# Two heads' float32 attention products side by side in the first two batches of a sink-attention and mixer kernel

## The chip, the core and the metric

One Trainium2 chip, one core of it. The metric is the device time of one execution in microseconds. Five engines matter here: TensorE (PE, with its weight loads shown apart as PEld), VectorE (DVE), ScalarE (ACT), GpSimd (POOL), and SyncE (SP), which issues nearly all transfers.

## What is computed

Attention with 4 sink keys and a window of 128 keys, for 4 batches, 8 heads, 768 positions and a head size of 64; its output goes through a mixer: a rank-32 mix along the sequence and a feed-forward layer of 2048.

```python
def _attn_ref(q, k, v, n_sink, window):          # q, k, v: (4, 8, 768, 64)
    scores = scale * np.matmul(q, k.transpose(0, 1, 3, 2))
    keep = is_sink | in_window                   # 4 sinks, 128 keys back
    scores = np.where(keep, scores, -1000000000.0)
    a = np.exp(scores - max); a = a / (sum(a) + 1e-09)
    return np.matmul(a, v)
def _moe_ref(x, U, V, w_ch1, w_ch2):             # x: (4, 768, 512)
    u = x + (xt @ U @ V).transpose(0, 2, 1)
    return u + np.maximum(u @ w_ch1, 0.0) @ w_ch2
```

The weights come as 64-bit floats and are turned into pairs of reduced float32 tiles (fp32r, a high and a low part) on the chip, in seven steps each (`narrow_steps`, L83).

## The kernel before

The order of the work is written out by a planner. Each piece is a step with an engine (or a choice of engines), an assumed duration, a priority and the tiles that it reads and writes (`Plan.any`, L246). A list scheduler runs forward and backward over all steps, picks an engine where there is a choice, and the steps are then issued in the order of their planned starts (`order`, L271). Its durations are the code's own entries, not measurements.

Batch 0's attention runs first, by halves of the sequence (`attention_halves`, L788): 2 halves of 384 positions, 8 heads each. Then batch 0's feed-forward runs (`spread`, L1021, and `ffn`, L950), during which the weights are narrowed for the first time and batch 1's attention is done beside it (`attention`, L773). Batch 2's attention lies beside batch 1's feed-forward, and so on. A gate lets head h of batch 1 start only when the feed-forward has reached its mark int(6 + 2.5 h) (`BESIDE`, L64, and L779).

One head and half (`attend`, L766) takes: three score products, one for each block of 128 queries, over 260 columns of keys (132 for the first block of the sequence); for each a masked minimum on DVE (L643) and an exponential on ACT (L648); the normalising (L663 to L693); three transposes (L702); two triangular maskings of the transposed tile (DVE L711, POOL L727); and the product with the values (L752), whose result is copied from a PSUM bank into the activations xT (line L462 on ACT, L463 on DVE, both in the helper `copy`).

`WHOLE` (L61) says which products are plain float32: all of batches 0 and 1. There the scores use one float32 matmul over 128 rows, of which 64 are the head and 64 are zeros that the host put there (L637). The values' matmul takes 128 columns of stationary operand, of which 64 are the head and the other 64 the next block, not used (L751); the copy takes the first 64 rows of the result (L759). Batches 2 and 3 use fp32r pairs instead (L640, L641) and are not touched.

Loads for the plain products are one q, one k and one v transfer per head (`load_qk`, L611, `prep_v`, L571); heads take the tiles kh, qs, vhl or kl, qkraw, opl by turns. The first two heads' q and k are loaded ahead of the plan (L1283 to L1289), with zeros set by DVE on the other 64 rows.

Of the kernel before, what the change touches and what calls it, by code (L numbers as in the profile page):

```python
# [21 lines left out]
P = 128  # L22
# [8 lines left out]
NS = 4  # L31
# [25 lines left out]
NP = 3  # L57
NXT = NPAIR + 1
PERIOD = 4.32
ACC = (0xFFFF, 0xFFFF, 0xFFFF, 0xFFFF)  # L60
WHOLE = {0: (0xFFFF, 0xFFFF), 1: (0xFF, 0xFF)}  # L61
# [13 lines left out]
def f32(ap):  # L75
    return ap.bitcast(F32)

# [341 lines left out]
def dve(n):  # L419
    return 0.069 + n * 1.042e-3  # L420
# [14 lines left out]
class Fast:  # L435
# [135 lines left out]
    def prep_v(self, b, h, blocks, t0, whole=False):  # L571
# [5 lines left out]
        if whole:  # L577
            t = self.opl() if h % 2 else self.vhl()
            flat = lambda: f32(t().rearrange("p n s d -> p (n s d)")[:, :(n + 1) * D])
            self.put(t, lambda: (flat().rearrange("p (n d) -> p n d", n=n + 1), self.v[b, h][:, k0:k1 + 1, :]), (n + 1) * 32768, t0 - 8)  # L580
            return t, flat, k0
# [5 lines left out]
        return t, None, k0  # L587
# [23 lines left out]
    def load_qk(self, b, h, halves, t0):  # L611

        if b == 0 and halves == (0, 0) and h < len(self.first):
            qr, kr = self.first[h]
            return qr, kr, None, 0, 0
        q0, q1 = halves[0] * CH, (halves[1] + 1) * CH
        k0, k1 = max(q0 // P - 1, 0) * SW, q1 // P * SW
        kr, qr = (self.kh(), self.qs()) if h % 2 else (self.kl(), self.qkraw())
        self.put(kr, lambda: (f32(kr()[:, :k1 - k0]), self.k[b, h][:, k0:k1]), (k1 - k0) * 512, t0 - 16)
        self.put(qr, lambda: (f32(qr()[:, :q1 - q0]), self.q[b, h][:, q0:q1]), (q1 - q0) * 512, t0 - 15)  # L620
        return qr, kr, None, q0, k0

    def scores(self, half, t0, acc, qs, kh, kl, qbase=0, kbase=0):
        nc, add = self.nc, self.plan.add
        p, mn, sm = self.p(), self.mn(), self.sm()
        for u in range(NBLK):
# [7 lines left out]
            def mms(st=st, q0=q0, k0=k0, wd=wd):  # L634
                qap = qs()[:, q0:q0 + P]
                if kl is None:
                    nc.tensor.matmul(  # L637
                        st()[:, :wd], f32(qap), f32(kh()[:, k0:k0 + wd]), start=True, stop=True)
                    return
                nc.tensor.matmul(st()[:, :wd], qap, kh()[:, k0:k0 + wd], start=True, stop=False)  # L640
                nc.tensor.matmul(st()[:, :wd], qap, kl()[:, k0:k0 + wd], start=False, stop=True)  # L641
            add("PE", 0.005 + wd / 600.0 if kl is None else mm(wd, 2), mms, r=[x for x in (qs, kh, kl) if x] + [(p, u)], w=(st,), prio=t0, after=self.gate)
            add("DVE", dve(wd), lambda st=st, u=u, lo=lo, wd=wd, qb=qb: nc.vector.tensor_tensor_reduce(  # L643
# [725 lines left out]
```

## Time and profile before

| | before |
|---|---|
| runs | 762.37, 762.2, 761.8 us; median 762.2 us |
| profiled execution | 760.85 us, of which the span (first to last instruction) is 759.1 us |
| PE busy | 745.9 us (98%) |
| DVE busy | 459.1 us (60%) |
| ACT busy | 353.4 us (47%) |
| POOL busy | 187.9 us (25%) |
| mean granted clock of TensorE | 0.998 |

Busy time counts the records of an engine; those of PE overlap in a stream, so the time that a matmul takes there is read from the distance between starts, not from its length. A record that says L462, L463, L469 or L471 belongs to a helper: the tile's name tells what it does. "x6" on a matmul's piece counts records, and a plain float32 matmul leaves two matmul records and two weight loads.

### The profile page before, as it was taken

What the parts mean: (1) busy time and instruction counts of PE and PEld (TensorE: products, weight loads), DVE (VectorE), ACT (ScalarE), POOL (GpSimd) and SP (SyncE); (2) the same over time, 40 slices, a digit from 0 to 9 for tenths busy, and PEclk for the clock granted to TensorE, in tenths of its full rate; (3) what the DMA queues carried; (4) which work ended last, traced back from release to release, by engine and by line L of the source; (5) the groups of instructions that cost most, each with busy time, mean ns of one, the idle gap of its engine ahead of it and who ended that gap; (6) DMA issues with size and microseconds to landing.
All of it is one profiled execution on the core that took longest, in us unless ns stands there. A gap on an engine that the chain in (4) does not pass through costs nothing.

```text
span 759.1 us, 11690 instructions
## 1 busy us (share of the span) xinstructions
PE 745.9 (98%) x4012; PEld 667.4 (88%) x4012; DVE 459.1 (60%) x1184; ACT 353.4 (47%) x1024; POOL 187.9 (25%) x288
## 2 busy tenths in 40 slices
PE   8999999999999999999999999999999999999997
PEld 6786998888888999999999989899999898989995
DVE  8989779898899586676853176766653131112111
ACT  6997367666676374564551155555542111111110
POOL 4761011223232344424611033522501000000000
PEclk9999999999999999999999999999999999999999
DMA  8898477773876478762586448761266527523752
GB/s 289 277 318 293 180 268 251 264 260 105 280 236 232 147 192 259 232 220 77 168 265 218 166 130 280 233 191 49 69 217 225 210 92 260 186 102 129 257 189 95
DMA packets 46981, 153.90 MB, mean 203 GB/s; under 512 B 5824, under 2 KB 13888, under 8 KB 37440
## 3 DMA queue, kind: packets, MB, share of 16 engines
q1 hardware_dynamic: 46752, 152.86, 60.7%
q8 instruction: 33, 0.54, 0.3%
q14 instruction: 36, 0.29, 0.1%
q10 hardware_dynamic: 160, 0.20, 0.1%
HBM read 123.42 MB, written 29.62 MB: 202 GB/s over the span
## 4 chain that ended last, share of the span: by engine, by line
PE 91%; DVE 5%; ACT 2%; issue 1%; POOL 0%; DMA 0%; POOLq 0%; DVEq 0%
PE bank L987 35%; PE bank L966 12%; PE bank L968 12%; PE bank L967 12%; PE bank L752 6%; PE bank L637 4%; PE bank L702 2%; PE bank L640 2%; PE bank L641 1%; PE bank L866 1%; DVE bank L101 1%; PE bank L1004 1%; ACT p L648 1%; DVE p L469 1%; PE bank L849 1%
## 5 line engine op out<-in xcount | busy, mean ns | idle before, releaser
L987 PE MATMUL bank<-w,hh 128*128 128x512 f32 x768 | 243.4, 398 | 0.0
L977 DVE SCALAR_TENSOR_TENSOR hl<-bank,hh 128x384 fp32r<-128x384 f32 x128 | 70.8, 553 | 189.2 <-ACT hh L974 188.7
L966 PE MATMUL bank<-ul,w 128*128 128x384 f32 x512 | 178.9, 349 | 0.0
L968 PE MATMUL bank<-uh,w 128*128 128x384 f32 x512 | 172.8, 337 | 0.0
L967 PE MATMUL bank<-uh,w 128*128 128x384 f32 x512 | 172.3, 337 | 0.0
L974 ACT ACTIVATE hh<-bank 128x384 fp32r<-128x384 f32 x119 | 58.4, 491 | 220.8 <-PE bank L968 219.9
L987 PEld LDWEIGHTS bank<-w,hh 128*128 128x128 f32 x768 | 139.3, 188 | 19.4
L987 PE MATMUL bank<-w,hl 128*128 128x512 f32 x384 | 152.3, 397 | 0.0
L648 ACT ACTIVATE p<-p,mn 128x260 f32<-128x260 f32 (+1 forms) x192 | 93.3, 487 | 41.0 <-DVE mn L643 40.5
L967 PEld LDWEIGHTS bank<-uh,w 128*128 128x128 f32 x512 | 96.4, 188 | 5.7
L966 PEld LDWEIGHTS bank<-ul,w 128*128 128x128 f32 x512 | 96.2, 188 | 5.7
L968 PEld LDWEIGHTS bank<-uh,w 128*128 128x128 f32 x512 | 96.0, 188 | 0.0
L987 PEld LDWEIGHTS bank<-w,hl 128*128 128x128 f32 x384 | 72.1, 188 | 17.7 <-DVE hl L977 1.1
L643 DVE CUSTOM_DVE_ANT_0 p<-bank,mask 128x260 f32<-128x260 f32 (+1 forms) x192 | 70.9, 400 | 17.6 <-PE bank L641 13.3
L682 POOL TENSOR_TENSOR p<-p,r 128x396 f32<-128x396 f32 x33 | 29.0, 878 | 113.1 <-DVE r L670 95.9
L471 POOL TENSOR_TENSOR ul<-xT,uh 128x384 fp32r<-128x384 f32 x15 | 15.1, 1022 | 122.0 <-ACT uh L462 84.8
L727 POOL TENSOR_SCALAR_AFFINE_SELECT oph<-oph 128x384 f32<-128x384 f32 (+1 forms) x64 | 36.3, 567 | 21.5 <-ACT oph L462 17.7
L471 POOL TENSOR_TENSOR p<-p 128x256 f32<-128x256 f32 (+1 forms) x22 | 19.2, 871 | 81.2 <-ACT p L648 77.7
L752 PEld LDWEIGHTS bank<-oph,vhl 128*128 128x128 f32 x224 | 35.8, 190 | 3.9 <-POOL oph L727 0.6
L752 PE MATMUL bank<-oph,vhl 128*128 128x256 f32 (+1 forms) x224 | 38.9, 303 | 0.0
L648 ACT ACTIVATION_READ_ACCUMULATOR p<-p,mn 128x1 f32 x192 | 36.1, 188 | 0.0
L702 PE MATMUL bank<-ident,p 128*128 128x128 f32 x192 | 33.3, 277 | 1.9 <-ACT p L680 1.5
(178 smaller groups left out, 1079.5 us busy)
## 6 DMA issues: line engine op xcount, KB each, us to landing
w<-wd SPq DMA_DIRECT2D x60, 1024.0 KB, 4.9
big<-in_w_dram SPq DMA_DIRECT2D x32, 512.0 KB, 5.4
wd<-w SPq DMA_DIRECT2D x14, 1024.0 KB, 4.8
big<-xd SPq DMA_DIRECT2D x33, 256.0 KB, 3.1
qkraw<-in_q_dram SPq DMA_DIRECT2D x39, 192.0 KB, 4.3
qkraw<-in_k_dram SPq DMA_DIRECT2D x32, 198.0 KB, 5.6
out_dram<-big SPq DMA_DIRECT2D x24, 256.0 KB, 2.1
v_raw<-in_v_dram SPq DMA_DIRECT2D x16, 192.0 KB, 2.8
```

The costliest lines, as they stand in the source:

```text
L471: ways["POOL"] = (gps(n), lambda: nc.gpsimd.tensor_tensor(dst(), a(), b(), op), True)
L643: add("DVE", dve(wd), lambda st=st, u=u, lo=lo, wd=wd, qb=qb: nc.vector.tensor_tensor_reduce(p()[:, u, NS + lo:], st()[:, :wd], self.mask[ ...
L648: add("ACT", act(wd) + 0.22, lambda u=u, lo=lo: nc.scalar.activation(p()[:, u, NS + lo:], p()[:, u, NS + lo:], AF.Exp, bias=mn()[:, u:u + ...
L702: nc.tensor.transpose(tr()[:, u * P:(u + 1) * P], p()[:, u, SW + NS:], self.ident)
L727: add("POOL", 0.126 + CH * 0.914e-3, lambda t=t: nc.gpsimd.affine_select(as_(t()[:, :, 1, :]), f32(t()[:, :, 1, :]), [[0, NBLK], [1, P]], ...
L752: nc.tensor.matmul(out, st, f32(mv) if whole else mv, start=part == 0 and i == 0, stop=part == len(t) - 1 and i == len(mms) - 1, skip_grou ...
L966: nc.tensor.matmul(ph()[:, :CH], wh, ul()[:, d, :], start=d == 0, stop=False)
L967: nc.tensor.matmul(ph()[:, :CH], wl, uh()[:, d, :], start=False, stop=False)
L968: nc.tensor.matmul(ph()[:, :CH], wh, uh()[:, d, :], start=False, stop=d == NC - 1)
L974: self.plan.any({"ACT": (act(CH), lambda: nc.scalar.activation(hh(), ph()[:, :CH], AF.Relu)), "DVE": (dve(CH), lambda: nc.vector.tensor_sc ...
L977: add("DVE", dve(CH), lambda: nc.vector.scalar_tensor_tensor(hl(), ph()[:, :CH], 0.0, f32(hh()), ALU.max, ALU.subtract), r=(ph, hh), w=(hl ...
L987: nc.tensor.matmul(acc[k](), a()[:, sl], w()[:, m, :], start=not begin and i == 0 and j == 0, stop=i == n - 1 and j == 2)
```

## The change

In batches 0 and 1 (`PAIRED = 2`) heads are handled two at a time. The host no longer pads with zeros: q and k come as 64 rows a head, and one transfer brings two heads into the 128 partitions, one on rows 0 to 63 and one on rows 64 to 127. A score step issues two matmuls, each over its own 64 rows, into two banks. A value step issues two matmuls for each key block, each with 64 stationary columns, whose results lie in one bank, one on partitions 0 to 63 and one on 64 to 127; one copy of 128 x 384 takes both to xT. The two tiles of probabilities are one of the ring p (3) and one of the ring qkraw (3); the two transposed tiles are oph and opl. Two transfers bring the values of a pair. The gate of a pair is that of its even head. The statistics tiles mn and sm become one tile ms in a ring of 7, the ring of r grows from 3 to 4, the other form of the sum (`acc` false, not in use) is dropped, and so are the zeros on DVE and a memset of p on POOL. The planner's entry for a score step goes from 0.005 + columns/600 us for one head to 0.105 + columns/600 us for two, that for a value step from 1.08 and 1.30 us for one head to 1.25 and 1.50 us for two.

```diff
+PAIRED = 2
-WHOLE = {0: (0xFFFF, 0xFFFF), 1: (0xFF, 0xFF)}
+def two_heads(x, b, pr):
+    return x[b, 2 * pr:2 * pr + 2].rearrange("h d n -> (h d) n")
...
+    def load_pair(self, b, pr, halves, t0):
+        if b == 0 and halves == (0, 0) and pr < len(self.first):
+            qr, kr = self.first[pr]
+            return qr, kr, 0, 0
...
+        kr, qr = self.kh(), self.qs()
+        self.put(kr, lambda: (f32(kr()[:, :k1 - k0]), two_heads(self.k, b, pr)[:, k0:k1]), (k1 - k0) * 512, t0 - 16)
+        self.put(qr, lambda: (f32(qr()[:, :q1 - q0]), two_heads(self.q, b, pr)[:, q0:q1]), (q1 - q0) * 512, t0 - 15)
...
+    def load_v_pair(self, b, pr, blocks, t0):
...
+        for i in range(2):
+            self.put(t, lambda i=i: (flat()[:, i * n * D:(i + 1) * n * D].rearrange("p (n d) -> p n d", n=n),
+                                     self.v[b, 2 * pr + i][:, k0:k1, :]), n * 32768, t0 - 8, part=i)
...
+    def attend_pair(self, b, pr, half, t0, qk, v, xT):
...
+        ps = [self.p(), self.qkraw(wide)]
+        sms = [self.ms(), self.ms()]
+        for u in range(NBLK):
...
+            sts = [self.bank(), self.bank()]
+            def mms(sts=sts, q0=q0, k0=k0, wd=wd):
+                for i, st in enumerate(sts):
+                    rows = slice(i * D, (i + 1) * D)
+                    nc.tensor.matmul(
+                        st()[:, :wd], f32(qr()[rows, q0:q0 + P]), f32(kr()[rows, k0:k0 + wd]), start=True, stop=True)
+            add("PE", 0.105 + wd / 600.0, mms, r=[qr, kr] + [(p, u) for p in ps], w=sts, prio=t0, after=self.gate)
+            for st, p, sm in zip(sts, ps, sms):
+                self.soften(st, p, sm, u, lo, wd, qb, t0)
+        ts = []
+        for i in range(2):
+            self.normalise(b, 2 * pr + i, half, t0 + i, ps[i], sms[i], self.sinks[b])
+            ts += self.transposes(half, t0 + i, ps[i], True, self.opl if i else self.oph)
+        pa = self.bank()
...
+            for j, (kb, lo, hi, c0) in enumerate(mms):
+                for i in range(2):
+                    mv = ts[i]().rearrange("p u s j -> p (u s j)")[:, lo * P:hi * P]
+                    at = (i * n + kb - kb0) * D
+                    nc.tensor.matmul(
+                        pa()[i * D:(i + 1) * D, c0 * P:(c0 + hi - lo) * P], flat()[:, at:at + D], f32(mv),
+                        start=j == 0, stop=j == len(mms) - 1, skip_group_check=True)
+        both = [(xT, (half, 0)), (xT, (half, 1))]
+        add("PE", (0.0, 1.25, 1.50)[len(mms) - 2], run, r=ts + [t] + both, w=(pa,), prio=t0)
+        self.copy(CH, lambda: xT()[:, half * CH:(half + 1) * CH], lambda: pa()[:, :CH], psum=True, r=(pa,), w=both, prio=t0)
...
+            if b < PAIRED:
+                if h % 2 == 0:
+                    pr = h // 2
+                    qk, v = self.load_pair(b, pr, (0, 1), t0), self.load_v_pair(b, pr, (0, NB), t0)
+                    for half in range(2):
+                        self.attend_pair(b, pr, half, self.t0(16 * b + 2 * (h + half)), qk, v, self.x[b][-1])
+                continue
...
-            nc.gpsimd.memset(tiles[-1][:, :, 0:NS], 0.0)
...
-            nc.sync.dma_start(kt[0:D, :NBLK * SW], k[0, h][0:D, :NBLK * SW])
-            nc.scalar.dma_start(qt[0:D, :CH], q[0, h][0:D, :CH])
-            nc.vector.memset(qt[D:P, :CH], 0.0)
-            nc.vector.memset(kt[D:P, :NBLK * SW], 0.0)
+            nc.sync.dma_start(kt[:, :NBLK * SW], two_heads(k, 0, pr)[:, :NBLK * SW])
+            nc.scalar.dma_start(qt[:, :CH], two_heads(q, 0, pr)[:, :CH])
```

## Rows read from the trace of the kernel before

**Rows 1.** The page: the chain that ended last, by engine.
```profile
PE 91%; DVE 5%; ACT 2%; issue 1%; POOL 0%; DMA 0%; POOLq 0%; DVEq 0%
```

**Rows 2.** Busy by stage: length, PE, PEld, DVE, ACT, POOL; clock, DMA share, GB/s.
```profile
5.28:76.00 70.72, 66.65 (x341) 52.80 (x342) 65.35 (x220) 60.63 (x203) 34.87 (x53) 1.00 0.91 309
14.80:31.70 16.90, 16.87 (x94) 14.51 (x95) 15.53 (x62) 16.80 (x68) 12.17 (x19) 1.00 0.88 275
53.00:76.00 23.00, 21.43 (x108) 15.80 (x107) 21.68 (x49) 17.72 (x45) 4.59 (x8) 1.00 0.86 304
76.00:241.00 165.00, 163.70 (x865) 145.95 (x864) 144.06 (x363) 104.07 (x276) 36.25 (x44) 1.00 0.68 228
217.00:226.00 9.00, 7.70 (x44) 6.53 (x43) 7.96 (x12) 6.63 (x18) 4.99 (x4) 1.00 0.47 161
```

**Rows 3.** The chain in order of time, batch 1: start us, us, piece.
```profile
109.91 1.09 PE bank L752 x6
...
112.22 1.31 PE bank L752 x8
...
115.45 1.10 PE bank L637 x6
...
135.24 1.32 PE bank L637 x6
```

**Rows 4.** The same view in batch 0's attention and up to its feed-forward.
```profile
26.85 0.44 PE bank L637 x2
...
61.65 0.69 DVE bank L102
...
73.35 0.47 DVE xT L942
```

**Rows 5.** Timeline of PE round a group of scores: start, length, operation.
```profile
101.46 2.58 PE L637 MATMUL bank<-kl,qkraw 128*128 128x132 f32 x12
103.68 0.53 PE L966 MATMUL bank<-ul,w 128*128 128x384 f32 x1
104.05 0.33 PE L967 MATMUL bank<-uh,w 128*128 128x384 f32 x1
104.22 0.34 PE L968 MATMUL bank<-uh,w 128*128 128x384 f32 x1
```

**Rows 6.** The values' weight loads, 76 to 245 us: count, ns min/median/max.
```profile
L752 PEld LDWEIGHTS bank<-oph,vhl x56: 187/190/192, 109.6 to 207.6; 128*128 128x128 f32 x56
```

**Rows 7.** Groups on ACT, 5 to 76 us and then 100 to 240: busy, mean ns.
```profile
L462 ACT COPY xT<-bank 64x384 f32<-64x384 f32 x14 | 6.6, 468 | 0.2
...
L462 ACT COPY xT<-bank 64x384 f32<-64x384 f32 x16 | 7.6, 473 | 6.4 <-PE bank L752 6.0
```

**Rows 8.** Groups on DVE, 100 to 240 us, that another engine could take.
```profile
L469 DVE TENSOR_TENSOR p<-p 128x384 f32<-128x384 f32 (+1 forms) x9 | 5.8, 647 | 0.3 <-ACT p L648 0.3
...
L97 DVE TENSOR_SCALAR nr<-nr 128x512 uint16<-128x512 uint16 x8 | 2.3, 284 | 0.1
L94 DVE TENSOR_SCALAR nr<-big 128x512 uint16<-128x512 uint16 x4 | 2.0, 493 | 0.0
```

**Rows 9.** Timeline of all engines at the start of the kernel.
```profile
1.26 0.57 SPq L1285 DMA_DIRECT2D first0k<-in_k_dram  x1
...
5.28 2.51 PE L637 MATMUL bank<-first0k,first0q 128*128 128x132 f32 x6 [0.68 <-DVE m_ck L155]
...
6.57 0.29 DVE L643 CUSTOM_DVE_ANT_0 p<-bank,mask 128x132 f32<-128x132 f32 x1 [0.27 <-DVE mask L160]
...
11.16 1.34 PE L637 MATMUL bank<-kl,qkraw 128*128 128x132 f32 x6 [1.63 <-DVE r L670]
```

**Rows 10.** Transfers issued in 0 to 10 us: KB each, us to landing.
```profile
kl<-in_k_dram SPq DMA_DIRECT2D x2, 198.0 KB, 4.3
...
first0k<-in_k_dram SPq DMA_DIRECT2D x1, 99.0 KB, 3.3
```

**Rows 11.** The chain at the end of batch 1's attention.
```profile
219.74 1.84 DVE nr L96
...
225.59 1.35 PE bank L752 x6
```

More of the change, by code (lines that the diff above doesn't have):

```diff
@@ L626, in scores @@
+    def scores(self, half, t0, qs, kh, kl, qbase=0, kbase=0):
+        nc, add = self.nc, self.plan.add
+        p, sm = self.p(), self.ms()
         for u in range(NBLK):
@@ L658, in scores, with soften @@
-        return p, sm
-    def past(self, p, u, lo):
-        return p()[:, u, 0:SW] if lo == 0 else p()[:, u, 0:1].broadcast_to([P, SW])
-    def normalise(self, b, h, half, t0, acc, p, sm, psink):
+            add("PE", mm(wd, 2), mms, r=[qs, kh, kl, (p, u)], w=(st,), prio=t0, after=self.gate)
+            self.soften(st, p, sm, u, lo, wd, qb, t0)
+        return p, sm
+    def soften(self, st, p, sm, u, lo, wd, qb, t0):
+        nc, add = self.nc, self.plan.add
+        add("DVE", dve(wd), lambda: nc.vector.tensor_tensor_reduce(
+            p()[:, u, NS + lo:], st()[:, :wd], self.mask[:, min(qb, 2), lo:],
+            -0.125, 3.0e38, ALU.add, ALU.min, sm()[:, u:u + 1]), r=(st,), w=((p, u), (sm, u)), prio=t0)
+        add("ACT", act(wd) + 0.22, lambda: nc.scalar.activation(
+            p()[:, u, NS + lo:], p()[:, u, NS + lo:], AF.Exp, bias=sm()[:, u:u + 1], scale=-1.0,
+            accum_out=sm()[:, NBLK + u:NBLK + u + 1]), r=((sm, u),), w=((p, u), (sm, NBLK + u)), prio=t0)
@@ new lines, in normalise, with scale @@
+        own, past = lambda: p()[:, u0:, SW + NS:], lambda: p()[:, u0:, NS:SW]
+        self.tt((NBLK - u0) * P, own, own, past, ALU.add, w=(p,), prio=t0)
+        def scale():
+            for u in range(NBLK):
+                nc.scalar.activation(p()[:, u, SW:], p()[:, u, SW:], AF.Copy, scale=r()[:, u:u + 1])
+        self.plan.any({"ACT": (NBLK * 0.3, scale),
+                       "POOL": (0.82, lambda: nc.gpsimd.tensor_tensor(kept(), kept(), by(), ALU.mult), True),
+                       "DVE": (dve(NBLK * SW), lambda: nc.vector.tensor_tensor(kept(), kept(), by(), ALU.mult), True)},
+                      r=(r,), w=(p,), prio=t0)
@@ L693, in normalise, with transposes @@
                       r=(p,), w=((psink, (half, h)),), prio=t0)
-    def transposes(self, half, t0, p, whole):
+    def transposes(self, half, t0, p, whole, own=None):
         nc, add = self.nc, self.plan.add
         tr = self.bank()
-        res = [self.oph()] if whole else [self.oph(), self.opl()]
+        res = [own()] if whole else [self.oph(), self.opl()]
         def mms():
```

155 lines of the change are left out of this document (57 added, 98 removed).

## The prediction

> **What bounds the kernel now.** I read the chain that ended last first: nine tenths of it lie on PE [rows 1], so a change of PE's own work can reach the end. But a chain that goes through PE does not say that PE alone is full, so I then read the table by stage [rows 2]. The reader is to see two stages there. From 5.28 to 76 us, batch 0's attention, PE, DVE and ACT are all nearly full: of 70.7 us DVE is busy 65.35 and ACT 60.63, and between 14.8 and 31.7 us ACT has 16.80 of 16.90. The chain in that stage runs over PE first and then mostly over DVE, up to the last operation ahead of the feed-forward, an addition into xT at 73.35 [rows 4]. From 76 to 241 us, batch 0's feed-forward with batch 1's attention and the narrowing of the weights beside it, PE is busy 163.70 of 165 and DVE 144.06, which is 87%. The fullest stretch of DVE is 53 to 76 us with 21.68 of 23, or 94%; I take that as what DVE can be filled to in this program. From 241 us on nothing is touched, and PE leaves no gap worth naming, so that part only moves.
>
> **What the plain products cost.** The pieces of the chain give distances in a stream. Three scores take 1.10 us in the first half and 1.32 in the second, the values 1.09 and 1.31 [rows 3]. One float32 matmul of 260 columns is two records and takes 0.44 us [rows 4], so a record takes 0.22 us, one of 132 columns 0.11 (from 1.10 less two times 0.44, halved), one of 256 columns 0.22 and one of 128 columns 0.11. Per batch: scores 8 x 2.42 = 19.4 us, values 8 x 2.40 = 19.2 us, together 38.6 us of PE in each of the two stages.
>
> **Scores and values by pairs.** The trace before has no two matmuls on parts of the array, so the price of a pair must be bounded. From above: the two run one after the other and nothing is saved (38.6). From below: they run wholly together, and one costs what one head's did (19.3). I take a value between, from the two records of each matmul: the order on PE is A1, A2, B1, B2, then the next pair. A2 has to follow A1 on the same part of the array. If matmuls start in their written order and only neighbours on different parts overlap, then A1 is alone, A2 runs beside B1, B2 beside the next A1. Three score pairs in a row then take 7 records' time for 12: 0.11 + 0.11 + 5 x 0.22 = 1.32 us in the first half and 7 x 0.22 = 1.54 in the second; pairs that stand alone between feed-forward matmuls take three records each, 1.65 and 1.98. Over 4 pairs of heads that is 11.4 to 14.5 us; the middle is 13. Values, always in a row: five records of 0.22 and two of 0.11 make 1.32, and in the second half 1.54, together 11.4 us. The planner's old entries (1.10 and 1.32 for three scores, 1.08 and 1.30 for the values) agree with the trace to 2% [rows 3]; its new ones add up to 12.1 and 11.0 us. That is only the code's own entry, no measurement, but it lies where this order of records puts it.
>
> Going from the whole array to parts of it and back may cost something, and no row has it. The nearest is the step from plain float32 to fp32r: behind a group of scores the next matmul starts 0.37 us before its successor, where 0.17 is usual [rows 5]. Such a step is there before and after. For the new kind I take half of its extra 0.2 us, and 0 and 0.2 as ends: 16 groups x 2 steps x 0.1 = 3.2 us a batch. PE work per batch is then 13 + 11.4 + 3.2 = 27.6 instead of 38.6: **11 us less**, between -6.4 (no overlap, 32 steps of 0.2) and 19.3.
>
> As to that step, the row above shows only a delay of 0.2 us after plain float32, at an unchanged shape. The Trainium skill (TensorEngine Tiling, Tiling Modes, Key Properties) says that changing the tiling mode drains the engine, which speaks against scattering 24 score pairs among the feed-forward's matmuls; no run here shows it. It gives no figure; with the upper end of 0.2 the saving would be 8 us rather than 11.
>
> **Batch 1's stage (76 to 241 us).** PE would need 165 - 11 = 154 us. DVE's 144.06 us would then fill 93.5% of it, against the 94% taken as its limit. So DVE is just able to follow, and I keep 10 of the 11 us. What relieves it: 16 copies of 0.47 us on ACT [rows 7] become 8 of the same 384 columns, 3.8 us of ACT, and ACT (104 of 165) can take the steps L94 and L97, POOL the sums L469, together 10 us of DVE [rows 8]. What is next behind PE is therefore DVE. The gate of a pair is its even head's, so the last release comes at mark 21 instead of 23; at the end of batch 1's attention PE idles 1.3 us of 9 behind DVE and POOL [rows 2, 11], and this earlier release is cover for it. The term is **10 us**, between 3 and 19.
>
> **Batch 0's stage (5.28 to 76 us).** PE gets the same 11 us back here, but it shares the limit with DVE and ACT, whose work per head is unchanged but for the copies: 16 become 8, worth 3.8 us at the 0.47 of [rows 7]. Of ACT's and DVE's 126 us that is 3%, and 3% of 70.7 us is 2.1. Besides, the third head's scores start only at 11.16 after PE sat idle 1.63 us [rows 9], and the first transfers now bring four heads instead of two. I take **3 us**, with 0 (the other engines hide it) and 5.4 (all of DVE's idle time) as ends. So most of the 11 us that PE saves here buys nothing.
>
> **Edits at nothing.** The zeros on DVE lie before it waits for the limits at the start, the memset of p on POOL before its first work. The first transfers carry twice the bytes: k is issued at 1.26 and took 3.3 us for 99 KB, while 198 KB took 4.3 [rows 9, 10], so it may land at 5.6, 0.3 us after the first score starts now; the first minimum on DVE waits at 6.57 for the mask anyway [rows 9]. Later transfers are fewer (28 for 44 in batch 0, 16 for 24 in batch 1) and half the bytes, which shortens SP's queue. A pair's value step waits for both heads' probabilities; behind it on PE stand feed-forward matmuls in batch 1 and other pairs in batch 0, and six tiles of probabilities instead of three keep heads in flight. The ring qkraw is also batch 2's, whose first loads come a stage later. If none of these covers held, I would put 1 us on them.
>
> **Sum.** 10 + 3 = 13 us from the profiled execution's 760.85 us (span 759.1 and 1.75 around it) is 747.9; the median of the runs is 1.35 us higher, so **749.2 us**.
>
> **Rivals.**
> - DVE takes the place of PE. If DVE is filled no better than in 217 to 226 us (7.96 of 9, 88.4%), its 144.06 us need 163, and batch 1's stage gives 2 us; with 2 from batch 0 the time is 758. For: DVE's margin in my sum is half a per cent, and one of its steps took 1.84 us there [rows 11]. Against: 10 us of its work can go elsewhere.
> - Whole overlap. Each pair costs what one head did and no step between shapes is paid: 19.3 us off PE, for which DVE must give 8 of the 10 us of [rows 8] away (136 / 0.943 = 144 us). With 4 from batch 0 the time is 739. For: the two matmuls share no rows, or no columns. Against: the second record of each must wait for the first.
> - **Slower: the pair does not overlap** on this engine for plain float32, so the change does not do what it says. PE then does the same 38.6 us and pays 32 steps of 0.1 to 0.2 us, 3.2 to 6.4 a batch; batch 0 hides its part behind the saved copies. That gives 764 to 769, say 766. It decides once a pair of 260 columns takes more than the 0.88 us of two singles. For: nothing in the trace shows an overlap. Against: nothing speaks for a loss of the order of the gain.
> - Values' weight loads come out from behind the matmuls. They take 190 ns each [rows 6] and now lie beside the stream, since a record takes 0.22. Per batch there are 112; with all of them bare, values cost 11.4 + 21.3 = 32.7 for 19.2, more than scores save (19.4 - 13 - 3.2 = 3.2). With batch 0 hiding half of its loss this gives 770. The Trainium skill (TensorE: Matmul & The Clock Gate, Part 3, The mechanism) says that weight loads overlap matmuls in flight only where the row group differs, and the two halves of a value step have the same rows. The trace before disagrees for plain matmuls, whose loads on the same rows are hidden.
>
> **How the numbers follow.** Forecast as summed (743 to 754): 0.50. DVE bound (754 to 761): 0.20. Whole overlap (736 to 743): 0.14. No overlap: 0.11. Bare loads: 0.05. The range of 8 in 10 is 738 to 760: all of the forecast, nearly all of the DVE case and most of the whole overlap. A change under 0.2%, 1.5 us, is about what a measurement cannot tell from none. Faster: 0.84; the same: 0.04 (edges of the DVE case and of no overlap); slower: 0.12.
>
> **What would show it.** A score pair alone at about 0.66 us, three in a row at 1.3 to 1.55, a value group at 1.3 and 1.55: right; near 0.44 for a pair: whole overlap; near 0.88: none. The feed-forward's first matmul at about 73 us instead of 76, and batch 1's first feed-forward 13 us earlier in all. DVE at 93 to 95% between them with PE still full; PE with more than 3 us of idle time there would be the DVE case. The forecast is wrong if the time from 241 us on changes, or if batch 0's stage shrinks by much more than 5 us.

## The result and the profile after

The changed kernel takes **753.5 us** (median of four runs, 753.26 to 755.71) against 762.0 for the kernel before on the same chip: a ratio of 0.9895, interval 0.9883 to 0.9908, or 8.0 us less by that ratio, which goes by the means (the medians differ by 8.5). That is faster, inside the range of 738 to 760, and 4.3 us above the forecast of 749.2. The execution that was profiled took 755.71 us, 2.0 to 2.5 more than the other three, with a span of 753.9. It is 5.1 us shorter than the profiled execution of the kernel before (760.85), so what is read from these two traces accounts for 5.1 us and not for 8.0.

The chain that ended last, by engine; PE has 81% of it where it had 91% [rows 1]:

```profile
PE 81%; DVE 12%; ACT 2%; DMA 2%; issue 1%; POOL 1%; SPq 0%; DVEq 0%; POOLq 0%; ACTq 0%
```

Busy time in the stretches of [rows 2] (length, PE, PEld, DVE, ACT, POOL; granted clock, DMA share, GB/s):

```profile
5.28:76.00 70.72, 61.73 (x378) 41.88 (x379) 66.83 (x225) 55.39 (x186) 34.07 (x54) 0.95 0.62 207
14.80:31.70 16.90, 14.11 (x109) 8.76 (x109) 16.88 (x71) 16.49 (x67) 13.50 (x24) 0.98 0.53 157
53.00:76.00 23.00, 22.04 (x113) 16.44 (x112) 21.87 (x43) 14.64 (x30) 4.43 (x4) 1.00 0.60 209
76.00:241.00 165.00, 159.02 (x860) 124.71 (x859) 149.32 (x376) 104.97 (x278) 39.97 (x52) 0.99 0.70 238
217.00:226.00 9.00, 9.00 (x46) 8.08 (x46) 8.93 (x19) 6.99 (x14) 2.68 (x2) 1.00 0.92 288
```

The reader is to see two things. From 14.8 to 31.7 us it is now PE that has room (14.11 of 16.9) and DVE that has none. And from 76 to 241 us, where PE had 1.3 us of idle time, it has 6.0, while DVE is at 149.32 of 165, or 90%.

**The pairs themselves.** Timeline of PE in a value step (start, length, operation):

```profile
18.85 0.43 PE L675 MATMUL bank<-oph,vhl 128*64 128x256 f32 x1
18.86 0.43 PE L675 MATMUL bank<-opl,vhl 128*64 128x256 f32 x1
19.12 0.38 PE L675 MATMUL bank<-oph,vhl 128*64 128x256 f32 x1
19.13 0.38 PE L675 MATMUL bank<-opl,vhl 128*64 128x256 f32 x1
19.34 0.38 PE L675 MATMUL bank<-oph,vhl 128*64 128x256 f32 x1
```

The records of the two heads start 0.01 us apart, and the next two follow after 0.21 to 0.26, the distance of one head's records before. So the pair runs wholly together; nothing is staggered. The same view round one pair of scores that stands among the feed-forward's matmuls:

```profile
98.89 0.34 PE L1007 MATMUL bank<-uh,w 128*128 128x384 f32 x1
99.07 0.33 PE L1008 MATMUL bank<-uh,w 128*128 128x384 f32 x1
99.33 0.71 PE L652 MATMUL bank<-kh,qs 64*128 64x260 f32 x4
99.97 0.45 PE L1006 MATMUL bank<-ul,w 128*128 128x384 f32 x1
100.25 0.34 PE L1007 MATMUL bank<-uh,w 128*128 128x384 f32 x1
```

Two heads' product over 260 columns takes 0.64 us from its start to the next, where two records beside each other would need 0.43: 0.21 more. The matmul ahead of it is followed after 0.26 and the one behind it after 0.28, where 0.17 to 0.18 is usual: 0.19 more. A run of pairs thus carries 0.4 us for its steps, half of it inside the run, against 0.2 behind a group before [rows 5]. Pieces of the chain (start, us, piece) show the same for two pairs in a row, 1.08 us (0.87 + 0.21), and 1.23 and 1.48 us for the values of two heads, where one head took 1.09 and 1.31 [rows 3]:

```profile
99.40 0.64 PE bank L652 x4
...
110.72 1.23 PE bank L675 x12
...
113.36 1.48 PE bank L675 x16
...
137.27 1.08 PE bank L652 x8
```

Weight loads of the values, 76 to 245 us (count, ns min/median/max; [rows 6] before), and the copies on ACT from 5 to 76 us and from 100 to 240 us (busy, mean ns; [rows 7] before):

```profile
L675 PEld LDWEIGHTS bank<-oph,vhl x56: 133/137/138, 110.6 to 203.5; 128*64 128x64 f32 x56
```

```profile
L467 ACT COPY xT<-bank 128x384 f32<-128x384 f32 x6 | 2.8, 475 | 1.1 <-PE bank L675 1.1
...
L467 ACT COPY xT<-bank 128x384 f32<-128x384 f32 x8 | 3.9, 481 | 1.0 <-PE bank L675 0.8
```

**The start.** PE's first score starts at 6.23 us, where it started at 5.28 [rows 9]. In both kernels it comes behind the masks' first operations on DVE, and these wait for the limits, a transfer of 2 KB issued at 0.81 us. Its issue before and after (KB, us to landing), and the first score after:

```profile
sc_raw<-in_limits_dram SPq DMA_DIRECT2D x1, 2.0 KB, 2.6
```

```profile
sc_raw<-in_limits_dram SPq DMA_DIRECT2D x1, 2.0 KB, 3.6
...
6.23 1.37 PE L652 MATMUL bank<-first0k,first0q 64*128 64x132 f32 x12 [1.63 <-DVE m_ck L160]
```

In all eleven kernels here that load by pairs this transfer took 3.4 to 4.0 us, in the three that do not 2.6. Beside it run the first transfers of q and k, which now carry 192 and 198 KB where they carried 96 and 99. That they hold it up fits, but no run varied them alone.

**Where the gain is reached and lost.** The weight matmuls of the feed-forward (L966 before, L1006 after) are the same in number and order, so the start of the n-th one can be compared. Timeline of PE, first, fourth, seventh and 34th step, first of the kernel before, then of the changed one:

```profile
76.40 0.34 PE L966 MATMUL bank<-ul,w 128*128 128x384 f32 x1
...
86.90 0.34 PE L966 MATMUL bank<-ul,w 128*128 128x384 f32 x1
...
100.94 0.34 PE L966 MATMUL bank<-ul,w 128*128 128x384 f32 x1
...
272.14 0.34 PE L966 MATMUL bank<-ul,w 128*128 128x384 f32 x1
```

```profile
67.26 0.34 PE L1006 MATMUL bank<-ul,w 128*128 128x384 f32 x1
...
84.38 0.44 PE L1006 MATMUL bank<-ul,w 128*128 128x384 f32 x1
85.15 0.44 PE L1007 MATMUL bank<-uh,w 128*128 128x384 f32 x1 [0.33 <-DVE w L474]
...
97.01 0.34 PE L1006 MATMUL bank<-ul,w 128*128 128x384 f32 x1
...
265.36 0.33 PE L1006 MATMUL bank<-ul,w 128*128 128x384 f32 x1
```

The first step starts 9.1 us earlier, but the fourth only 2.5: it waits for weights that DVE is still narrowing. At the start of the seventh, just ahead of batch 1's first scores in either kernel, the lead is 3.9 us, and at the 34th, behind batch 1's attention, 6.8. So batch 0's stage gave 3.9 us, and batch 1's 2.9; by the fourth step it would be 2.5 and 4.3. Behind the 34th step the lead shrinks again, to 5.2 us at the end of the span.

To see what became of PE's saving I added up the distances between the starts of successive records on PE from 5 us to that 34th step, each counted to the record that it begins with, and idle time by itself (in us; `full_array` is an experiment below, taken up to its own 34th step):

```
                                     before   after   full_array
scores and values, batches 0 and 1     77.4    50.0         75.3
feed-forward matmuls                  141.5   148.1        142.6
transposes                             11.3    14.5          9.9
all other matmuls                      31.7    32.7         31.9
PE idle                                 5.1    13.8          7.8
```

The work is the same: up to that step both kernels have 1365 matmul records, and DVE is busy 231 us in both (length, PE, PEld, DVE, ACT, POOL; granted clock, DMA share, GB/s):

```profile
5.00:272.14 267.14, 261.50 (x1365) 226.93 (x1366) 231.19 (x629) 179.03 (x513) 82.31 (x107) 1.00 0.72 243
```

```profile
5.00:265.36 260.36, 245.11 (x1365) 188.74 (x1365) 231.16 (x637) 171.08 (x493) 78.69 (x112) 0.98 0.65 222
```

The products got 27.4 us shorter. Of that 8.7 us came back as idle time, 6.6 in the feed-forward's matmuls, 3.2 in the transposes and 1.0 in the rest, 19.5 in all; the later start takes another 1.0. Sorted by the engine that ended it, the idle time is 8.3 us behind DVE (2.4 before), 3.6 behind POOL (0.7) and 2.0 behind ACT (2.0). Its largest waits, in the view of PE's waits from 5 to 241 us (who for whom: us, times, longest):

```profile
PE bank L745 <- POOL qkraw L729: 2.3, 5, 0.7
...
PE bank L1027 <- DVE hl L1017: 2.2, 2, 2.0
PE bank L652 <- DVE ms L704: 2.1, 2, 1.5
...
PE bank L1007 <- DVE w L474: 1.4, 5, 0.3
PE bank L745 <- POOL p L729: 1.3, 2, 0.8
```

No single wait is over 2.0 us, and there are many short ones.

The waits cost more than this idle time. Idle time counts from the end of the record ahead, while in a stream the next record starts before that end: at 84.38 above the next start comes after 0.77 us, where 0.18 is usual, and 0.33 of it count as idle. So I sorted the records of the feed-forward and of the transposes by where they stand, and added up what each takes over the median of its kind and shape: next to an idle stretch 4.6 us (0.2 in the kernel before), next to an attention product 5.8 (4.0), in the stretches with a lower clock below 2.6 (none), elsewhere 1.4 (1.2). Of the 19.5 us that came back, 13 are thus waits, some 3 lie where the clock was low, and 2 are steps into and out of the runs of pairs.

Three stretches (columns as above) show a granted clock of 0.50, the lower of TensorE's two levels (1.2 GHz), in the changed kernel:

```profile
12.00:15.00 3.00, 3.00 (x16) 2.12 (x12) 2.60 (x15) 2.21 (x9) 1.92 (x4) 0.50 0.72 233
50.00:52.00 2.00, 2.00 (x14) 1.12 (x11) 1.89 (x3) 1.19 (x3) 1.93 (x3) 0.50 0.06 25
238.00:240.00 2.00, 1.92 (x5) 1.18 (x5) 1.96 (x4) 0.29 (x1) 0.00 (x0) 0.50 0.40 120
```

With their edges they are about 10 us long in all, which bounds their price, idle time and products included, at half of that, 5 us. Each came behind waits of PE: in the three us ahead of them (8.9 to 11.9, 46.4 to 49.4 and 234.2 to 237.2 us) PE was busy 1.55, 1.99 and 1.21 us. The profiled execution of the kernel before shows 1.00 in each stage [rows 2]. But executions differ in this: the changed kernel's other three have a mean granted clock of 0.994 to 0.997 where this one has 0.992, and those of the kernel before, timed beside the experiments, 0.993 to 0.999. So the clock can explain only little of what the medians lack.

Behind the 34th step, where nothing was changed, the kernel takes 488.5 us to the end of the span, and the kernel before 487.0. The feed-forward's 2003 records there take 407.4 us instead of 404.9, spread thinly and without idle time. `full_array` has 407.5, so this comes with the pairs' kernel and not with the overlap; its cause stays open.

### The profile page after: what moved, and what is told of

The parts are those of the page before. It is cut to its first block, busy times and chain, and to the rows that moved or that the text cites. A ratio compares the mean times of both kernels' runs of the same rounds, so it can differ in the third digit from the quotient of the medians.

```text
span 753.9 us, 11587 instructions
## 1 busy us (share of the span) xinstructions
PE 731.2 (97%) x4012; PEld 631.0 (84%) x4012; DVE 453.9 (60%) x1168; ACT 341.4 (45%) x977; POOL 193.5 (26%) x316
## 4 chain that ended last, share of the span: by engine, by line
PE 81%; DVE 12%; ACT 2%; DMA 2%; issue 1%; POOL 1%; SPq 0%; DVEq 0%; POOLq 0%; ACTq 0%
PE bank L1027 32%; PE bank L1006 11%; PE bank L1007 11%; PE bank L1008 11%; PE bank L793 3%; PE bank L652 2%; PE bank L745 2%; PE bank L675 2%; DVE nr L104 2%; PE bank L695 1%; PE bank L696 1%; DVE w L474 1%; DVE bank L106 1%; PE bank L906 1%; DVE xT L982 1%
## 5 line engine op out<-in xcount | busy, mean ns | idle before, releaser
L1027 PE MATMUL bank<-w,hh 128*128 128x512 f32 x768 | 246.5, 402 | 1.2 <-ACT hh L1014 0.6
L1006 PE MATMUL bank<-ul,w 128*128 128x384 f32 x512 | 178.9, 349 | 0.3 <-ACT w L467 0.2
L1006 PEld LDWEIGHTS bank<-ul,w 128*128 128x128 f32 x512 | 96.6, 189 | 11.9 <-issue 3.4
L707 ACT ACTIVATE p<-p,ms 128x132 f32<-128x132 f32 (+1 forms) x144 | 69.9, 487 | 33.3 <-DVE ms L704 32.7
L704 DVE CUSTOM_DVE_ANT_0 p<-bank,mask 128x132 f32<-128x132 f32 (+1 forms) x144 | 54.3, 401 | 13.3 <-PE bank L696 10.8
L467 ACT COPY tb<-bank 64x384 f32<-64x384 f32 x31 | 14.7, 474 | 40.1 <-PE bank L793 40.0
L729 POOL TENSOR_TENSOR p<-p,r 128x396 f32<-128x396 f32 x27 | 24.2, 898 | 31.9 <-DVE r L718 25.5
L474 DVE TENSOR_TENSOR xT<-bank,tb 64x384 f32<-64x384 f32 x32 | 17.6, 549 | 23.1 <-ACT tb L467 22.8
L770 POOL TENSOR_SCALAR_AFFINE_SELECT oph<-oph 128x384 fp32r<-128x384 f32 (+1 forms) x48 | 27.2, 568 | 13.7 <-ACT oph L467 11.1
L770 POOL TENSOR_SCALAR_AFFINE_SELECT opl<-opl 128x384 fp32r<-128x384 f32 (+1 forms) x48 | 26.1, 544 | 7.4 <-ACT opl L467 4.1
L745 PE MATMUL bank<-ident,p 128*128 128x128 f32 x144 | 25.2, 281 | 2.5 <-POOL p L729 1.3
```

What stands on the lines that cost most here:

```text
L474: ways = {"DVE": (dve(n), lambda: nc.vector.tensor_tensor(dst(), a(), b(), op), pool)}
L704: add("DVE", dve(wd), lambda: nc.vector.tensor_tensor_reduce(p()[:, u, NS + lo:], st()[:, :wd], self.mask[:, min(qb, 2), lo:], -0.125, 3.0 ...
L707: add("ACT", act(wd) + 0.22, lambda: nc.scalar.activation(p()[:, u, NS + lo:], p()[:, u, NS + lo:], AF.Exp, bias=sm()[:, u:u + 1], scale=-1.0,
L745: nc.tensor.transpose(tr()[:, u * P:(u + 1) * P], p()[:, u, SW + NS:], self.ident)
L770: add("POOL", 0.126 + CH * 0.914e-3, lambda t=t: nc.gpsimd.affine_select(as_(t()[:, :, 1, :]), f32(t()[:, :, 1, :]), [[0, NBLK], [1, P]], ...
L1006: nc.tensor.matmul(ph()[:, :CH], wh, ul()[:, d, :], start=d == 0, stop=False)
```

## The experiments

Ratios are to the kernel before, timed beside it on the same chip. Three questions were open: how much the overlap itself is worth, whether DVE took the place of PE, and how the gain depends on the size of PE's saving.

**Is it the overlap?** In the first two runs one batch's pairs are issued in the changed kernel's order, but as matmuls that use the same part of the array one after the other. The edit for batch 0 (for batch 1 with `b == 1`):

```diff
-                    rows = slice(i * D, (i + 1) * D)
+                    rows = slice(0, D) if b == 0 else slice(i * D, (i + 1) * D)
...
+                    if b == 0:
+                        at = min(at, (2 * n - 2) * D)
+                        nc.tensor.matmul(
+                            pa()[:, c0 * P:(c0 + hi - lo) * P], flat()[:, at:at + P], f32(mv),
+                            start=i == 0 and j == 0, stop=i == 1 and j == len(mms) - 1, skip_group_check=True)
+                        continue
```

> The changed kernel in its own order, but in batch 0 the two matmuls of a score pair both use rows 0 to 63, and those of a value step both use all 128 columns, so nothing runs side by side there (the second head's products are not its own). Theory 'DVE': after the change the stretch up to 240 us is bound by VectorE with the narrowing of the weights, so PE's saving in batch 0 is mostly given back while the first feed-forward steps wait for their weights; the time rises by 1 to 4 us from the changed kernel's 753.5. Theory 'PE': what was missing went to steps between array shapes and to a lower clock on PE, PE still sets the time, and the whole 9 us by which the feed-forward started earlier is lost: +8 to +10 us.

> The same in batch 1 alone, beside batch 0's feed-forward. PE gets some 14.7 us of work more in that stage (38.6 before, 23.9 now by the chain). Theory 'DVE': DVE hides part of it; +5 to +9 us from 753.5. Theory 'PE': +13 to +15 us.

Measured: 769.2 us, 1.0077 (1.006 to 1.0094), and 768.17 us, 1.007 (1.0053 to 1.0086). Against the changed kernel that is 14 and 13 us for one batch each, more than the 8.0 that both batches bring. So the overlap is needed. But the first number, above what either theory expected, is not its worth: the clock fell too. Two stretches of `one_part_b0`, then 8 to 26 us in `full_array`, which does these products one after the other over the whole array:

```profile
8.00:26.00 18.00, 18.00 (x53) 13.97 (x53) 12.06 (x61) 10.71 (x46) 7.03 (x13) 0.50 0.48 158
28.00:31.00 3.00, 3.00 (x17) 2.54 (x16) 1.80 (x8) 2.24 (x10) 2.85 (x5) 1.00 0.13 35
```

```profile
8.00:26.00 18.00, 16.73 (x94) 14.29 (x93) 16.79 (x87) 16.75 (x71) 9.97 (x17) 1.00 0.65 212
```

In `one_part_b0` PE left no gap in 18 us, mostly with scores over 64 rows, and was granted 0.50 throughout; the clock is at 1.00 again in the second stretch, behind values over the whole array. Timeline of PE there: twelve score records in 4.71 us.

```profile
19.39 4.71 PE L652 MATMUL bank<-kh,qs 64*128 64x132 f32 x12
```

In `one_part_b1` the clock did not fall where the edit is:

```profile
76.00:241.00 165.00, 162.03 (x811) 134.00 (x810) 138.48 (x350) 99.97 (x269) 36.86 (x50) 1.00 0.65 219
```

Its 13 us are what "PE" expected (13 to 15) and not what "DVE" did (5 to 9). Time that is put onto PE in this stage, in an order that was made for shorter products, counts nearly in full, so PE still sets the stage's length there. What less time on PE would bring is not shown by it.

The same edit for both batches, with the planner told the longer times:

```diff
-            add("PE", 0.105 + wd / 600.0, mms, r=[qr, kr] + [(p, u) for p in ps], w=sts, prio=t0, after=self.gate)
+            add("PE", 0.105 + 2 * wd / 600.0, mms, r=[qr, kr] + [(p, u) for p in ps], w=sts, prio=t0, after=self.gate)
...
-        add("PE", (0.0, 1.25, 1.50)[len(mms) - 2], run, r=ts + [t] + both, w=(pa,), prio=t0)
+        add("PE", (0.0, 2.30, 2.75)[len(mms) - 2], run, r=ts + [t] + both, w=(pa,), prio=t0)
```

> Both batches' pairs on one part of the array (as in one_part_b0 and one_part_b1 together), with the planner's entries raised to twice the columns, so that the order fits. It keeps the pairs' loads, copies and tiles and loses only the overlap. If the overlap alone carries the gain, 765 to 772 (before's PE work plus the steps between shapes, less the saved copies); if pairing itself costs some 20 us, as the two runs in a fixed order add up to, about 780.

Measured: 783.68 us, 1.0285 (1.0259 to 1.0311), a little above the second expectation. In batch 0 it is spoilt by the clock in the same way, and the column of the granted clock can't be trusted at its start. It says 1.00 from 25 to 30 us (first fence), but the timeline of PE (second fence) has two value records of 256 columns in 0.85 us, twice the 0.21 of above:

```profile
25.00:30.00 5.00, 5.00 (x14) 3.92 (x14) 2.69 (x13) 0.99 (x3) 1.48 (x2) 1.00 0.33 97
```

```profile
26.38 1.06 PE L677 MATMUL bank<-opl,vhl 128*128 128x256 f32 x2
27.23 1.06 PE L677 MATMUL bank<-oph,vhl 128*128 128x256 f32 x2
```

**Did DVE take PE's place?** If it did, taking work off DVE must help the changed kernel and not the one before. The edit cuts one of the seven narrowing steps to 8 columns, in either kernel:

```diff
-        ({"DVE": lambda: v.scalar_tensor_tensor(a(), top(), 0x8000, a(), ALU.bitwise_and, ALU.bitwise_or)}, "raw", "a"),
+        ({"DVE": lambda: v.scalar_tensor_tensor(a()[:, :8], top()[:, :8], 0x8000, a()[:, :8], ALU.bitwise_and, ALU.bitwise_or)}, "raw", "a"),
```

> The changed kernel in its own order, but one of the seven narrowing steps (the sign, 0.70 us on 128 x 512) handles 8 columns instead of all, so weights lose their signs; some 0.64 us x 32 = 20 us of VectorE's time up to 240 us is gone and nothing else. Theory 'DVE': the waits for weights and the late masks shrink, 7 to 12 us faster than 753.5. Theory 'PE': 0 to 3 us faster.

> The same cut of VectorE's time in the kernel before. Theory 'DVE': there PE is full from 76 us on, so only the first stage's end, whose last stretch is a chain on VectorE, comes earlier: 2 to 5 us faster than 762.0, clearly less than in the changed kernel. Theory 'PE': the same 0 to 3 us as in the changed kernel.

With the order left as it was: 749.97 us, 0.983 (0.9814 to 0.9846), in the changed kernel, and 758.76 us, 0.995 (0.9934 to 0.9967), in the one before. That is 4.9 us less than the changed kernel has and 3.8 less than the one before: no difference that tells the theories apart, and the first lies between the two ranges expected. A shorter step shortens the waits on it in both. Then with the planner told of it (the step's entry becomes 0.077 us):

```diff
-        cost = (0.069 + n * 0.52e-3, 0.069 + n * 0.26e-3, 0.069 + n * 0.26e-3, dve(n), 0.069 + n * 0.26e-3, dve(n), dve(n))
+        cost = (0.069 + n * 0.52e-3, 0.069 + n * 0.26e-3, 0.069 + n * 0.26e-3, 0.077, 0.069 + n * 0.26e-3, dve(n), dve(n))
```

> As after_less_dve (the sign step of the narrowing on 8 columns, weights without signs), but the planner is told the shorter step, so that all engines' orders are made anew. Theory 'DVE': the pairs' gain is held back by the order that VectorE's load forces on the planner, not only by waits in a given order; with 20 us less of it the changed kernel falls by 8 to 13 us, to 742 to 747. Theory 'PE': shape steps and the lower clock hold it back, VectorE matters as little as in the fixed order; 748 to 752.

> The same in the kernel before. Theory 'DVE': PE is full there, so a new order has little to win: 757 to 763. Theory 'PE': it gains as much as the changed kernel does.

Measured: 749.65 us, 0.9832 (0.9815 to 0.9849), and 763.17 us, 1.0009 (0.9996 to 1.0022): 4.8 us less than the changed kernel, 0.7 more than the one before. The first lies in the range of "PE" (748 to 752). It looks as if DVE cost the changed kernel some 5 us that it did not cost the one before, but that is not shown: with the same work the kernel before took 758.76 us in its old order, so the new order alone lost 4.5 us there (its 34th step starts at 275.37 us, and at 269.67 in the old order). Shown is that this work of DVE is worth about 5 us to the changed kernel in either order, and to the kernel before 3.8 in one order and nothing in the other. It also shows that a new order by itself can move these kernels by some 4 us. Timeline of PE, start of the 34th feed-forward step, and the stage from 76 to 241 us, both of the changed kernel with less DVE work:

```profile
258.45 0.33 PE L1006 MATMUL bank<-ul,w 128*128 128x384 f32 x1
```

```profile
76.00:241.00 165.00, 161.82 (x900) 133.65 (x899) 141.95 (x379) 99.90 (x268) 44.02 (x58) 0.99 0.70 240
```

The 34th step is now 13.7 us earlier than in the kernel before, instead of 6.8, and PE's idle time in the stage is 3.2 us instead of 6.0; DVE is at 86%. But the pair products still save 26.0 us there (51.4 instead of 77.4), and half of that is still missing. Up to the 34th step PE now idles 1.4 us behind DVE, where it was 8.3, but 7.3 behind ACT, where it was 2.0. So the waits moved to the next engine: DVE is one cause and not the only one.

**Can DVE's work go to POOL?** A kernel that does the whole computation, with batch 1's second masking triangle on POOL:

```diff
-        if whole:
+        if whole and not pool:
...
+        elif whole:
+            self.copy(CH, lambda: f32(top()), v3, psum=True, r=(tr,), w=((res[0], 1),), prio=t0)
...
-            if not whole:
+            if not whole or pool:
```

> The changed kernel with one of the two triangular maskings of batch 1 moved from VectorE (16 steps of 0.49 us on the PSUM bank) to GpSimd (on the copied tile, as batches 2 and 3 do it). It computes the whole reference. Theory 'DVE': 8 us less on VectorE in the stage, GpSimd has room; 2 to 4 us faster than 753.5. Theory 'PE': no change, or slower by the longer chain from transposes to values (0.5 us for each of 16).

Measured: 758.1 us, 0.9948 (0.9931 to 0.9964): 4.0 us slower than the changed kernel. The stage from 76 to 241 us shows why that says nothing on DVE:

```profile
76.00:241.00 165.00, 160.59 (x875) 127.27 (x874) 149.16 (x368) 104.79 (x277) 47.20 (x67) 1.00 0.69 237
```

POOL has 7 us more, but DVE has 149.16 as before (149.32): wherever there is a choice the planner filled DVE up again. The relief that was to be tried did not take place. Nearly all of the loss lies ahead of the moved work: the fourth step starts at 88.32 us, 3.9 later than in the changed kernel. The new order can do that, and so can the clock, whose mean is 0.988 to 0.991 in these executions.

**Is the gain in proportion, or does it stop at a next limit?** Three kernels keep the pairs' loads, copies, rings and gates, but do some products over the whole array one after the other, with the planner told so. The first edit does that to the scores, the second to the values. `full_array` has both, `scores_only` (only the scores stay side by side) the second, `values_only` the first:

```diff
-                    rows = slice(i * D, (i + 1) * D)
+                    rows = slice(0, P)
...
-            add("PE", 0.105 + wd / 600.0, mms, r=[qr, kr] + [(p, u) for p in ps], w=sts, prio=t0, after=self.gate)
+            add("PE", 0.01 + 2 * wd / 600.0, mms, r=[qr, kr] + [(p, u) for p in ps], w=sts, prio=t0, after=self.gate)
```

```diff
-                    at = (i * n + kb - kb0) * D
+                    at = min((i * n + kb - kb0) * D, (2 * n - 2) * D)
...
-                        pa()[i * D:(i + 1) * D, c0 * P:(c0 + hi - lo) * P], flat()[:, at:at + D], f32(mv),
-                        start=j == 0, stop=j == len(mms) - 1, skip_group_check=True)
+                        pa()[:, c0 * P:(c0 + hi - lo) * P], flat()[:, at:at + P], f32(mv),
+                        start=i == 0 and j == 0, stop=i == 1 and j == len(mms) - 1, skip_group_check=True)
...
-        add("PE", (0.0, 1.25, 1.50)[len(mms) - 2], run, r=ts + [t] + both, w=(pa,), prio=t0)
+        add("PE", (0.0, 2.16, 2.60)[len(mms) - 2], run, r=ts + [t] + both, w=(pa,), prio=t0)
```

> The pairs' loads, tiles, copies and order, but every matmul of a pair uses the whole array: scores over all 128 rows (which adds the two heads up), values with 128 stationary columns; the planner's entries are those of two heads one after the other, so PE has before's work, without steps between shapes and without half-filled arrays. If pairing as such is neutral: 759 to 763. If pairing itself costs time, which the one-part run (783.7) left open because its clock also fell: 768 or more.

> The changed kernel with the values on the whole array (two heads one after the other, planner's entries 2.16 and 2.60) and the scores side by side: PE keeps only the scores' saving, about 13 us of 27 over both batches. Theory 'next bound' (once PE gives some microseconds back, VectorE and what hangs on it set the stage's end): nearly the whole gain remains, 753 to 757. Theory 'in proportion to PE's work': half of the gain, 757.5 to 759.5.

> The other half: scores on the whole array (they add two heads up), values side by side; PE keeps about 16 us of the 27. Theory 'next bound': 753 to 757. Theory 'in proportion': 756.5 to 758.5.

Measured:

```
                side by side       us      ratio (95%)               from before, us
full_array      nothing            764.84  1.0029 (1.0017 to 1.0042)   +2.2
scores_only     scores             759.45  0.9960 (0.9944 to 0.9976)   -3.0
values_only     values             759.88  0.9954 (0.9938 to 0.9970)   -3.5
changed kernel  scores and values  753.5   0.9895 (0.9883 to 0.9908)   -8.0
```

Working by pairs without any overlap costs 2.2 us. From there the scores bring 5.2, the values 5.7 and both 10.2, close to their sum of 10.9 within the intervals (0.9 to 1.2 us to either side). If PE had only been freed up to a next engine's limit, the second half would have brought much less than the first. It brought nearly as much (5.0 for the values behind the scores, 4.5 the other way round): the two halves add up. In proportion to PE's time they are not: from `full_array` to the changed kernel the scores got 9.8 us shorter and the values 15.5, and `values_only` is 1.4 us above the range of "in proportion", `scores_only` at its edge. Each of these kernels has an order of its own, so that the sum comes out so well can be partly luck. In PE's own account it is 10.2 us at the end for 25.3 us of shorter products (75.3 to 50.0), two fifths. Stage from 76 to 241 us of `full_array`, and its 34th step, which starts 1.25 us later than in the kernel before:

```profile
76.00:241.00 165.00, 163.60 (x862) 146.25 (x861) 143.64 (x360) 102.64 (x270) 41.56 (x55) 1.00 0.65 221
```

```profile
273.39 0.33 PE L1006 MATMUL bank<-ul,w 128*128 128x384 f32 x1
```

PE and DVE stand as in the kernel before (163.70 and 144.06, [rows 2]) and the clock is at 1.00. It is the control that the one-part runs were meant to be. Its 764.84 us lie between the two expectations (759 to 763, or 768 and more). Part of this cost can be placed in the profiled executions, which differ by 3.8 us: its first score starts 0.65 us later than in the kernel before (5.93), and from the 34th step to the end of the span it takes 2.3 us longer (489.3).

**More of the same?** A kernel that does the whole computation with pairs in all four batches:

```diff
-PAIRED = 2
+PAIRED = 4
```

> The changed kernel with all four batches by pairs in plain float32 (PAIRED = 4); it computes the whole reference. In batches 2 and 3 this takes away the splitting of q, k and v into high and low parts and one of two transposed tiles (some 30 us of VectorE per batch), while PE's work there stays about the same (two records of fp32r of 0.12 us each per head against 0.64 us or less for a pair). VectorE has room there, so the theory 'VectorE holds back the first 240 us' says about the same time as the changed kernel, 752 to 755; if the copies and splits delay PE there too, 748 to 751.

Measured: 766.26 us, 1.0044 (1.0026 to 1.0062), some 11 us slower than the changed kernel, where 748 to 755 was expected. Busy time from 241 to 500 us, where batch 2's attention and most of batch 3's lie:

```profile
241.00:500.00 259.00, 258.57 (x1440) 215.12 (x1440) 103.86 (x310) 100.41 (x312) 50.18 (x82) 1.00 0.51 174
```

PE is as full as before, with much less work on the other engines (DVE 103.86 us). The products that were replaced there are reduced-float32 ones, which were not slow in the way that the plain ones were, and scattered pairs carry their steps of 0.4 us each. By the distances of the records behind the 34th step the attention products take 44.8 us there and 45.2 in the changed kernel, so nothing is saved, while the feed-forward's records take 413.4 instead of 407.4 and the transposes 9.1 instead of 8.0. PE idles less than 0.1 us behind that step, so nothing hides this. Another 3.4 us are lost before: the 34th step starts at 268.72 us instead of 265.36, again in a new order, with 12 attention records more ahead of it.

## Why the prediction was right or wrong

**Faster, and by what.** Right: PE's own work bounded the kernel, and less of it reached the end. Not right in size: 8.0 us instead of 13. That the time still lies in the range is partly luck, since two errors pull against each other: PE saved more than I said, and less of it reached the end.

**The mechanism of the pair.** Wrong. I had the two records of each matmul staggered, A1, then A2 beside B1, then B2 beside the next A1. They run wholly together, starts 0.01 us apart; there the rival of whole overlap was right. The cost came out near my numbers all the same, because a run of pairs carries steps: for a pair alone 0.64 us (forecast 0.66), for value groups 1.23 and 1.48 (1.3 and 1.55). By the distances of the records PE's products take 13.3 us (scores, in 17 runs) and 10.7 us (values) in batch 1, 24.1 instead of 38.6; over both batches it is 13.7 us less a batch (half of 27.4). The forecast had 11. So PE saved more than I said, and the kernel gained less.

**Steps between shapes.** The price that I took, about 0.1 us a step, is what the rows show: 0.4 us a run where 0.2 was before. The Trainium skill (TensorEngine Tiling, Tiling Modes, Key Properties) says that a change of the tiling mode drains the engine; the trace agrees with a cost of that kind, and this is its size.

**Weight loads.** They stayed behind the matmuls: 137 ns each, and the value records still follow after 0.21 us. The rule of the Trainium skill (TensorE: Matmul & The Clock Gate, Part 3, The mechanism) that a load overlaps only where the row group differs is not borne out here, for two halves of the columns on the same rows; the same section also lets a load into a background buffer go ahead, and no run here tells whether these do. My price for bare loads was summed wrongly: its own terms give about 778 us and not 770.

**Batch 0's stage.** The term of 3 us was about right at 3.9 (2.5 at the fourth step), by another way than I said. The feed-forward starts at 67.26 us, not at 73, since PE, freed, was put ahead of DVE. It then waits for the narrowing on DVE. Looked at alone, the early start would have said that the prediction was three times too low.

**Batch 1's stage is the step that failed**: "DVE is just able to follow, and I keep 10 of the 11 us". It gave 2.9 us (4.3 from the fourth step on). The error lies in how I asked the question. I held DVE's load of the whole stage (93.5% of 154 us) against the fullest stretch that I found (94%), and as it came out just below, I let nearly all pass. But there is no such sill. DVE stands at 90% over the stage while PE idles 6.0 us, and at 8.93 of 9 us from 217 to 226 us; PE waits on single operations of DVE, POOL and ACT long before any of them is full on the average, and 13 of the 19.5 us that came back are such waits. Nor did the relief come that I counted on, 10 us of DVE's work for ACT and POOL: up to the 34th step DVE is busy 231 us in both kernels. The experiments agree: the two halves of the gain add up (5.2 + 5.7 against 10.2 us), and less work on DVE gives 4.8 us and moves the waits to ACT. The rival "DVE takes PE's place" was right about its place (754 to 761 was its range, the measured time lies at its edge, and its own sign, over 3 us of idle time on PE, came with 6.0), and wrong about its kind: a sill at 88% would have stopped the second half of the gain.

**Costs put at nothing.** Working by pairs as such costs 2.2 us (`full_array`); I had put 1 us on it at most, and only if the covers failed. One did: I watched the first k against the mask on DVE, and the limits, for which the mask waits, land a us later themselves.

**The clock** was in no step. In the profiled execution the changed kernel loses at most 5 us to it in three stretches, each behind waits of PE. No run changed this by itself, but executions of one kernel give a scale: of `values_only`, three with a mean clock of 0.999 took 758.8 to 759.7 us, and three with 0.991 to 0.993 took 760.1 to 760.5. So its share of the missing gain is bounded and not measured.

**From 241 us on** I said that the part only moves, and that a change there would prove the forecast wrong. It changed a little: 1.5 us more from the 34th step to the end, which is open. What stays open too is why the planner's orders place the waits as they do; each experiment with a new order mixes that in.

**No overlap, slower** fell at once: the rival needed more than 0.88 us for a pair, and it took 0.64.

## What to carry to other kernels

Where several engines are each over 85% busy, don't test a saving on one of them against the fill that the next one can reach; its waits grow before that. Here two fifths of what the overlap took off PE's products reached the end. And where an experiment slows an operation down on purpose, read the clock before its time: the form that stands for "no overlap" has to keep the clock where it was. And where a planner makes the order anew, its choice alone can be as large as the effect: here some 4 us.

## What was not expected of the hardware

- Two plain float32 matmuls on different halves of the rows, or of the columns, run wholly side by side: starts 0.01 us apart, 0.64 us for two products of 260 columns, steps included, where one alone took 0.44.
- A run of such pairs among matmuls over the whole array carries about 0.4 us: 0.1 ahead, 0.2 inside, 0.1 behind.
- PE was busy 18.00 of 18 us, mostly with scores over 64 rows, at a granted 0.50 in `one_part_b0`, and 16.73 of 18 us over the whole array at 1.00 in `full_array`.
- A transfer of 2 KB took 3.4 to 4.0 us to land instead of 2.6 in the kernels whose first transfers beside it are twice as large.
